# A two-layer attention and gMLP kernel: helper transfers dealt over more steps, and seven stores moved from SP to POOL

## The chip, the cores and the metric

The kernel runs on one core of one Trainium2 chip. The core has five engines with queues of their own: TensorE (PE, matrix products; PEld is its loading of weights), VectorE (DVE), ScalarE (ACT), GpSimd (POOL) and SyncE (SP, which here only issues transfers). Transfers between DRAM and on-chip memory run on 16 DMA engines; an engine's queue issues them in its own order. POOL issues transfers too, among them those that add into what lies at the destination.

The metric is the device time of one execution in microseconds (us), as the median of several runs.

## The reference

Input is x, 2048 tokens by 512. Each of two layers, with the same weights, does a linear attention and a gated MLP whose gate mixes the tokens:

```python
x = x + A(layernorm(x))     # twice: A, B, A, B
x = x + B(layernorm(x))

def B(x):                                   # D = 512, Fh = 896, S = 2048
    z = gelu(x @ w_in)                      # [S, 2*Fh]
    z1, z2 = z[:, :Fh], layernorm(z[:, Fh:])
    g = w_sp @ z2 + b_sp[:, None]           # w_sp is [S, S]
    return (z1 * g) @ w_out
```

A projects to q, k and v in 32 heads of 16, applies `phi(t) = t+1 if t>0 else exp(t)`, sums k with v over all tokens, multiplies with q, divides by the normaliser and projects with wo. The change touches the mixing product `w_sp @ z2`, the storing of z1 and the transfers around them.

## The kernel before, in words

**Arithmetic.** Every fp32 product is made of three matmuls on a high part and a low part (L163 to L165 and L1484 to L1486: high by high, high by low, low by high). The high part is a rounded copy (type fp32r), the low part is what is left. For a piece of w_sp the copy is made on ACT (L1316) and the subtraction on DVE (L1317).

**Stages.** Each layer runs: layernorm, keys, values and their sums; a transition; a pass over the tokens that ends in x @ w_in and the gelu; then the mixing product with the gates, and the output product with w_out. The pages of z1 = gelu(x @ w_in1), 7 for each of four chunks of 512 tokens, are stored to DRAM (L991) and loaded again when the gates need them.

**The mixing product** is written in seven half-size products in place of eight: P2, P1, P6, P7, P4, P5, P3, in this order, 8 steps each. A step multiplies with one piece of w_sp of 512 KB, or with a sum of pieces. Some of these products are divided once more by the same scheme: P4 in layer one, P2 and P4 in layer two. A divided product has 14 steps of 12 matmuls: seven inner products 1, 5, 6, 2, 7, 3, 4 in two halves each (steps 0 and 1 are inner product 1, steps 2 and 3 inner product 5, and so on).

**What each step does.** `run` (L1786 and after) goes through the steps g. In step g:
- `fetch(g + 4)` issues the load of a piece on SP. A plain piece comes from w_sp itself (L1296, `qd<-in_wsp_dram`), an inner product's sum from the DRAM tiles hP (L1296, `qd<-hP`), an outer sum from the tiles s (L1301, `qd<-s`).
- `sp(g + 2)` splits the piece of step g + 2 (L1316 on ACT, L1317 on DVE). ACT's instruction is kept as `mark`.
- `mm(g)` issues the matmuls.
- one gate, where one is due, is issued (`tick`), a copy or an add of the list PARTS (`halve`), and, at the ends of products, the sums are taken out of PSUM by DVE (`evac`, `evac_div`).

A tile of a piece (raw) and its two parts (high and low together) come out of six slots, `qd`. A slot is free when the last reader is done: DVE's subtraction for the raw piece, the matmuls for the parts. So SP's next load often waits for a subtraction of DVE.

**Copies and adds for the sums.** hP holds the sums of pieces that the divided products need: for P4 and for P2, inner products 1, 3, 2 and 4 in two halves q. `halve(n)` does part n of 32, in layer one only: parts 0 to 7 are the copies for P4 (products 1, 3, 2, 4, two halves each), 8 to 15 the adds for P4 in the same order, 16 to 23 the copies for P2, and 24 to 31 its adds. A copy is a transfer of 512 KB from DRAM to DRAM, issued by SP (L1217). An add is an adding transfer of 512 KB, issued by POOL (L1221) behind `mark`. The adds for products 2 and 4 read hP of products 1 and 2. `PARTS` says at which step of which product each part is issued. The sums of P4 are used in the same layer, in its own P4; those of P2 and P4 are used again in layer two.

**The start of the mixing product in layer two.** The x @ w_in products of the last chunk (n = 3) run on into `run`: `while p2.f()` issues them, seven of them, each with its gelu into a page out of the pool `pg` (L988) and its store by SP (L991). After the fourth, `sp(1)` and `fetch(3)` are called. `loadb` loads four pages of b_sp (L1515) at step 0 of the mixing product in layer two, and at step 3 in layer one. The four slots `bg` serve as the sums gb[0] to gb[3], one for each chunk; in P2 the first sum written into gb[3] is that of inner product 5, behind step 3.

**The output stage** (`out7`) has eight rounds j. In each PE multiplies with parts of w_out, ACT and DVE take out the results, and `ofinish` adds pages of them into x by POOL's adding transfers (L1704). In layer one, `join_a` and `join_b` start layer two's loads and layernorm meanwhile (L133 loads its weights and x).

Of the kernel before, what the change touches and what calls it, by code (L numbers as in the profile page):

```python
# [15 lines left out]
P = 128  # L16
# [4 lines left out]
NCHK = S // 512  # L21
NF = FH // P
# [40 lines left out]
EXTRA = (2, 3, 4, 5, 16, 17)  # L63
WSTORE = 9
FS = {6: 1, 12: 1, 17: 1}
PARTS = {("P1", k): k - 2 for k in range(2, 8)} | {("P6", k): 6 + k for k in range(8)}
PARTS |= {("P7", 0): 14, ("P7", 1): 15} | {("P4", 2 * k): 16 + k for k in range(7)}
PARTS |= {("P4", 13): 23} | {("P5", k): 24 + k for k in range(8)}


class Sheets:
# [18 lines left out]
def mixer_kernel(ctx: ExitStack, tc: tile.TileContext, x_in, wqkv, wo_d, win1_d, win2_d, wsp_d, bsp_d, wout_d,  # L90
                 ident_d, mask_d, out_d):
    nc = tc.nc
# [7 lines left out]
    pages = Slots(main, "pg", 22)  # L100
    quads = Slots(main, "qd", 6)
    bigs = Slots(main, "bg", 4)
# [5 lines left out]
    def ztag(i, shape, kind, dtype=F32):  # L108
        t = main.tile(shape, dtype, tag=f"z{i}", bufs=1, name=f"z{i}_{kind}")
        ztile[i] = t  # L110
        return t
# [17 lines left out]
    z1s = {}  # L129
# [37 lines left out]
    class Weight:  # L167


        def __init__(self, slots, shape, pieces, turned=False):  # L170
            self.slots, self.shape, self.pieces, self.turned = slots, shape, pieces, turned
            self.h = self.l = None
            self.raw = deque()
            self.n_load = self.n_split = 0
# [147 lines left out]
    class ZHome:  # L322
# [3 lines left out]

        def get(self, shape, dtype=F32):
            return ztag(self.i, shape, "y" if dtype == F32 else "q", dtype)

        def put(self, t):  # L330
            pass
# [361 lines left out]
    class P2:  # L693
# [288 lines left out]
        def fout(self):  # L982
            if self.fdone is None:
                return
            b, n, f, home = self.fdone
            self.fdone = None
            t = home.get(PAGE)
            nc.scalar.activation(t, b, AF.Gelu_apprx_tanh)  # L988
            banks.put(b)
            z1s[self.L, n, f] = dram.tile(PAGE, F32, name=f"z1_{self.L}_{n}_{f}")  # L990
            nc.sync.dma_start(z1s[self.L, n, f], t)  # L991
            home.put(t)

        def run(self, sums):
# [260 lines left out]
    class P4:  # L1255
# [471 lines left out]
        def out7(self, nxt):  # L1727

            V = nc.vector
            lo, hi = slice(0, 256), slice(256, 512)  # L1730
            last = HT - 1
            u, y, z = self.begun
            for j in range(HT):
                if j == last - 1 and nxt is None:
                    self.loadx(NT - 2)
                    self.loadx(NT - 1)
                d, s = banks.get(PAGE), pages.get(PAGE)
                c = s[:, lo]
                more = j < last
                if more:  # L1740
                    self.opart(j + 1)
                    self.ohigh(0, 1, 2)
                    self.olow(0, 1, 2)
                    if j:
                        self.omul(z, 2, u[:, lo], False, True)
                    self.omul(z, 5, u[:, hi], False, True)
                    if j == 0:
                        self.omul(z, 2, u[:, lo], False, True)
                    nc.scalar.activation(c, u[:, hi], AF.Copy)
                    self.osum(1, 3)  # L1750
                else:
                    self.omul(z, 2, u[:, lo], False, True)
                if nxt is not None:
                    self.join_a(j, nxt)
                self.omul(z, 6, y[:, lo], False, False)
                nc.scalar.activation(d[:, lo], y[:, lo], AF.Copy)
                if more:
                    up, yp, zp = self.pair(j + 1)
                else:
                    self.omul(z, 5, u[:, hi], False, True)  # L1760
                    nc.scalar.activation(c, u[:, hi], AF.Copy)
                V.tensor_add(y[:, lo], y[:, lo], c)
                if more:
                    self.osum(2, 4)
                    self.ohigh(3)
                self.omul(z, 7, d[:, lo], False, False)
                V.tensor_add(d[:, hi], d[:, lo], c)
                pages.put(s)
                if more:
                    self.olow(3)  # L1770
                if j == 0:
                    self.evac("P3", (1,))
                for _ in range((0, 2, 1, 1, 2)[j] if j < 5 else 0):
                    self.tick()
                if nxt is not None:
                    self.join_b(j, nxt)
                self.omul(z, 3, y[:, lo], False, True)
                if more or nxt is not None:
                    self.omul(z, 4, d[:, lo], False, True)
                    self.ofree(z)  # L1780
                self.olone(j, 0, u[:, lo], lo)
                self.olone(j, 0, y[:, lo], hi)
                self.olone(j, 1, d)
                if more or nxt is not None:
                    self.ofinish(2 * j, (u[:, lo], lo), (y[:, lo], hi))
                    self.ofinish(2 * j + 1, (d, slice(0, 512)))  # L1786
                    banks.put(u, y, d)
                    pages.put(self.ones.pop(j))
                    if j % 2 == 0 and more:
                        bigs.put(self.gb[j // 2])  # L1790
                if more:
                    u, y, z = up, yp, zp
            if nxt is not None:
                return
            self.omul(z, 4, d[:, lo], False, True)
            self.olast(NT - 2, u[:, lo], lo)
            self.olast(NT - 2, y[:, lo], hi)
            self.olast(NT - 1, d[:, hi], hi)
            self.olast(NT - 1, d[:, lo], lo)
# [8 lines left out]
        def run(self, nxt):  # L1808
            p2 = self.p2
            self.fetch(2)  # L1810
            self.sp(0)
            self.zmade = 0
            if self.div:
                self.zahead(1)
            early = nxt is None
            n = 0
            while p2.f():
                self.zahead(min(self.zmade, 3))
                n += 1
                if early and n == 4:  # L1820
                    self.sp(1)
                    self.fetch(3)
            self.zahead(3)
            if p2.win1 is not None:
                p2.win1.free()
            if not early:
                self.sp(1)
                self.fetch(3)
            self.gb = [bigs.get([P, NF, 512]) for _ in range(NCHK)]
            n = len(self.steps)  # L1830
            for g in range(n):
                p, k = self.steps[g]
                self.fetch(g + 4)
                evac_first = (p == "P6" or p == "P1" and nxt is not None) and k == HT - 1
                div_first = p in self.div and k == 13 and p == "P4"
                if not evac_first and not div_first:
                    self.sp(g + 2)
                    self.zahead(g + 4 if p in ("P2", "P1") else g + 4)
                self.mm(g)
                if evac_first:  # L1840
                    if p == "P1":
                        self.ask(3)
                    self.evac(p)
                    self.sp(g + 2)
                self.sums.tick()
                if nxt is not None:
                    self.sums.halve(PARTS.get((p, k), -1), self.mark)
                if g == (0 if early else 3):
                    self.loadb()
                if p in self.div:  # L1850
                    if k % 2 == 1:
                        self.evac_div(p, self.SEVEN[k // 2])
                    if div_first:
                        self.sp(g + 2)
                    if k == 13 and p == "P4":
                        self.gq.extend((n, f) for n in range(2) for f in range(3))
                    continue
                if p == "P1" and k == 6:
                    self.ask(3)
                self.tick()  # L1860
                if p == "P3":
                    if k == FIRST:
                        self.first()
                self.wseven(p, k)
                if p == "P7" and k == HT - 1 and self.div:
                    self.sp(g + 3)
                if k == HT - 1 and not evac_first:
                    self.evac(p, (0,) if p == "P3" else (0, 1))
            pages.put(*self.bs)
            self.out7(nxt)  # L1870
# [34 lines left out]
    for L in range(2):  # L1905
        p1.run(sums)
        p2 = P2(p1)
# [5 lines left out]
        nxt = P1(1) if L == 0 else None  # L1913
# [33 lines left out]
```

## Time and profile before

| what | us |
|---|---|
| median of 3 runs | 1366.25 |
| lowest and highest run | 1366.12, 1369.26 |
| profiled execution, device time | 1368.58 |
| its span, first to last instruction | 1366.7 |
| busy PE, PEld | 1356.0, 1153.0 |
| busy DVE, ACT, POOL | 982.1, 695.6, 424.6 |

The profile is of one execution. In its rows a line such as L1317 is a line of the kernel before, `out<-in` names tiles, and `x7` counts instructions. A row of the timeline gives the start and the duration in us; brackets give the idle time just before and what ended it. PE is one after the other in matmuls whose stated durations overlap, so the distance between their starts tells its pace. A row of a wait gives total, times and longest. A DMA row gives the times from issue to landing.

### The profile page before, as it was taken

What the parts mean: (1) busy time and instruction counts of PE and PEld (TensorE: products, weight loads), DVE (VectorE), ACT (ScalarE), POOL (GpSimd) and SP (SyncE); (2) the same over time, 40 slices, a digit from 0 to 9 for tenths busy, and PEclk for the clock granted to TensorE, in tenths of its full rate; (3) what the DMA queues carried; (4) which work ended last, traced back from release to release, by engine and by line L of the source; (5) the groups of instructions that cost most, each with busy time, mean ns of one, the idle gap of its engine ahead of it and who ended that gap; (6) DMA issues with size and microseconds to landing.
All of it is one profiled execution on the core that took longest, in us unless ns stands there. A gap on an engine that the chain in (4) does not pass through costs nothing.

```text
span 1366.7 us, 18857 instructions
## 1 busy us (share of the span) xinstructions
PE 1356.0 (99%) x6602; PEld 1153.0 (84%) x6602; DVE 982.1 (72%) x1550; ACT 695.6 (51%) x1152; POOL 424.6 (31%) x573
## 2 busy tenths in 40 slices
PE   9999999999999999999999999999999999999998
PEld 7888888888888787889988888888887888888898
DVE  6665867762474688898866777777537768888985
ACT  5764534434322355354676655556676333644454
POOL 3753355444350400301322333545330022011021
PEclk9999999999999999999999999999999999999999
DMA  5872257877996968973664423678767445464444
GB/s 181 271 243 95 89 186 261 284 263 242 313 317 222 275 188 273 262 237 68 143 159 131 122 87 99 205 246 260 227 196 230 149 162 163 143 193 154 147 75 65
DMA packets 155022, 260.63 MB, mean 191 GB/s; under 512 B 13104, under 2 KB 52272, under 8 KB 154672
## 3 DMA queue, kind: packets, MB, share of 16 engines
q1 hardware_dynamic: 140240, 228.50, 50.6%
q0 software_dynamic: 14688, 30.94, 11.4%
q8 instruction: 51, 0.84, 0.2%
q14 instruction: 43, 0.35, 0.1%
HBM read 187.83 MB, written 88.34 MB: 202 GB/s over the span
## 4 chain that ended last, share of the span: by engine, by line
PE 75%; DVE 4%; DMA 3%; ACT 2%; issue 1%; POOL 0%; DVEq 0%; SPq 0%; ACTq 0%; POOLq 0%
PE bank L1484 11%; PE bank L1485 11%; PE bank L1486 11%; PE bank L165 9%; PE bank L163 9%; PE bank L164 9%; PE bank L1682 3%; PE bank L1683 3%; PE bank L1684 3%; PE bank L849 1%; PE bank L848 1%; PE bank L847 1%; DVE qd L1317 1%; DMA qd<-hP 1%; DMA pg<-z 1%
## 5 line engine op out<-in xcount | busy, mean ns | idle before, releaser
L1484 PE MATMUL bank<-qd,pg 128*128 128x512 f32 x776 | 302.4, 390 | 2.2 <-ACT pg L1354 1.8
L1485 PE MATMUL bank<-qd,pg 128*128 128x512 f32 x776 | 302.2, 389 | 1.4 <-DVE qd L1317 1.4
L1486 PE MATMUL bank<-qd,pg 128*128 128x512 f32 x776 | 302.1, 389 | 0.0
L1317 DVE TENSOR_TENSOR qd<-qd,qd 128x1024 fp32r<-128x1024 f32 x130 | 164.4, 1265 | 122.4 <-ACT qd L1316 122.4
L1316 ACT ACTIVATE qd<-qd 128x1024 fp32r<-128x1024 f32 x130 | 137.3, 1056 | 186.7 <-PE bank L1486 119.7
L165 PE MATMUL bank<-qd,pg 128*128 128x512 f32 x496 | 193.5, 390 | 0.3 <-DVE pg L152 0.3
L1484 PEld LDWEIGHTS bank<-qd,pg 128*128 128x128 f32 x776 | 145.6, 188 | 34.1 <-ACT pg L1354 2.6
L1485 PEld LDWEIGHTS bank<-qd,pg 128*128 128x128 f32 x776 | 145.7, 188 | 32.1 <-DVE qd L1317 2.1
L1486 PEld LDWEIGHTS bank<-qd,pg 128*128 128x128 f32 x776 | 145.7, 188 | 31.0 <-DVE pg L1356 0.7
L163 PE MATMUL bank<-qd,pg 128*128 128x512 f32 x356 | 138.8, 390 | 0.0
L164 PE MATMUL bank<-qd,pg 128*128 128x512 f32 x356 | 138.7, 390 | 0.0
L1525 POOL TENSOR_TENSOR bg<-bg,pg 128x512 f32<-128x512 f32 x28 | 51.4, 1837 | 246.5 <-ACT qd L1316 203.7
L165 PEld LDWEIGHTS bank<-qd,pg 128*128 128x128 f32 x496 | 93.1, 188 | 20.6 <-DVE pg L152 1.2
L298 POOL TENSOR_SCALAR rs<-mv 128x1 f32<-128x1 f32 x80 | 24.4, 304 | 214.8 <-DVE mv L296 213.3
L307 ACT ACTIVATE pg<-pg,nb,rs 128x512 f32<-128x512 f32 x52 | 42.1, 810 | 88.0 <-POOL nb L301 87.4
L1684 PE MATMUL bank<-wo,qd 128*128 128x256 f32 x288 | 81.4, 283 | 0.0
L1231 POOL TENSOR_TENSOR pg<-pg,pg 128x512 f32<-128x512 f32 x48 | 68.6, 1428 | 36.4 <-DMA pg<-in_wsp_dram 19.6
L164 PEld LDWEIGHTS bank<-qd,pg 128*128 128x128 f32 x356 | 66.8, 188 | 14.0 <-DVE qd L152 0.3
L163 PEld LDWEIGHTS bank<-qd,pg 128*128 128x128 f32 x356 | 66.8, 188 | 13.8 <-ACT pg L149 0.2
L1682 PE MATMUL bank<-wo,qd 128*128 128x256 f32 x276 | 78.1, 283 | 0.0
L1683 PE MATMUL bank<-wo,qd 128*128 128x256 f32 x276 | 78.0, 283 | 0.0
L1354 ACT ACTIVATE pg<-pg 128x384 fp32r<-128x384 f32 (+1 forms) x32 | 18.5, 579 | 84.6 <-DVE pg L1352 47.6
(224 smaller groups left out, 3071.8 us busy)
## 6 DMA issues: line engine op xcount, KB each, us to landing
qd<-s SPq DMA_DIRECT2D x64, 512.0 KB, 3.7
qd<-in_wsp_dram SPq DMA_DIRECT2D x42, 512.0 KB, 4.3
pg<-z SPq DMA_DIRECT2D x56, 256.0 KB, 4.0
pg<-w POOLq DMA_DIRECT2D x56, 256.0 KB, 4.9
pg<-in_wsp_dram SPq DMA_DIRECT2D x48, 256.0 KB, 5.0
z<-pg SPq DMA_DIRECT2D x48, 256.0 KB, 3.3
s<-pg SPq DMA_DIRECT2D x48, 256.0 KB, 4.4
qd<-hP SPq DMA_DIRECT2D x24, 512.0 KB, 3.8
```

Source lines behind the costliest of these rows:

```text
L163: nc.tensor.matmul(out, ah, bh, start=start, stop=False)
L164: nc.tensor.matmul(out, ah, bl, start=False, stop=False)
L165: nc.tensor.matmul(out, al, bh, start=False, stop=stop)
L1231: nc.gpsimd.tensor_tensor(t, a, b, op=OP.add)
L1316: self.mark = nc.scalar.activation(w[:, 0], r, AF.Copy)
L1317: nc.vector.tensor_sub(w[:, 1], r, w[:, 0].bitcast(F32))
L1484: m(out, h[:, o], w[:, 0, j, :], start=start, stop=False, skip_group_check=True)
L1485: m(out, h[:, o], w[:, 1, j, :], start=False, stop=False, skip_group_check=True)
L1486: m(out, l[:, o], w[:, 0, j, :], start=False, stop=stop, skip_group_check=True)
L1682: m(out, A, x, start=start and f == 0, stop=False, skip_group_check=True)
L1683: m(out, A, y, start=False, stop=False, skip_group_check=True)
L1684: m(out, B, x, start=False, stop=stop and f == 2, skip_group_check=True)
```

## The change

Three things change, and no transfer, matmul or other operation is added or taken away.

- `PARTS`: the 32 parts of copies and adds are dealt out anew. Parts 0 to 5 stay at P1's steps 2 to 7. Before, P6 had one part at each of its 8 steps, P7 one at steps 0 and 1, P4 one at steps 0, 2, 4, 6, 8, 10, 12 and 13, P5 one at each of its 8 steps. After, P6, P7 and P5 have one at steps 0, 2, 4 and 6, P4 one at the same steps as before, and the output stage one in each of the rounds 1 to 6. So the copies of P4's product 4 stand at P6's steps 0 and 2; the adds of product 1 at P6's 4 and 6, of product 3 at P7's 0 and 2, of product 2 at P7's 4 and 6, of product 4 at P4's 0 and 2; the copies for P2 at P4's 4, 6, 8, 10, 12, 13 and P5's 0 and 2; the adds for P2's product 1 at P5's 4 and 6, and the other six in the output stage.
- In layer two the last seven gelus write seven sheets of one `bg` slot (class `Spare`) in place of pages out of `pg`, and their stores are issued by POOL. The slot goes back before the four sums take their slots, and becomes gb[3].
- In layer two `loadb` moves from step 0 of the mixing product to the place behind the fourth of the last gelus, right after `fetch(3)`.

```diff
-PARTS = {("P1", k): k - 2 for k in range(2, 8)} | {("P6", k): 6 + k for k in range(8)}
-PARTS |= {("P7", 0): 14, ("P7", 1): 15} | {("P4", 2 * k): 16 + k for k in range(7)}
-PARTS |= {("P4", 13): 23} | {("P5", k): 24 + k for k in range(8)}
+PARTS = {}
+for p, ks in (("P1", range(2, 8)), ("P6", (0, 2, 4, 6)), ("P7", (0, 2, 4, 6)), ("P4", (0, 2, 4, 6, 8, 10, 12, 13)),
+              ("P5", (0, 2, 4, 6)), ("out", range(1, 7))):
+    for k in ks:
+        PARTS[p, k] = len(PARTS)
...
+    class Spare:
+
+        def __init__(self, t):
+            self.t, self.n = t, 0
+
+        def get(self, shape):
+            self.n += 1
+            return self.t[:, self.n - 1]
 
         def put(self, t):
             pass
...
             z1s[self.L, n, f] = dram.tile(PAGE, F32, name=f"z1_{self.L}_{n}_{f}")
-            nc.sync.dma_start(z1s[self.L, n, f], t)
+            (nc.gpsimd if self.L and n == NCHK - 1 else nc.sync).dma_start(z1s[self.L, n, f], t)
             home.put(t)
...
                 if nxt is not None:
                     self.join_b(j, nxt)
+                if nxt is not None:
+                    self.sums.halve(PARTS.get(("out", j), -1), self.mark)
                 self.omul(z, 3, y[:, lo], False, True)
...
             early = nxt is None
             n = 0
-            while p2.f():
+            spare = Spare(bigs.get([P, NF, 512])) if early else pages
+            while p2.f(home=spare):
                 self.zahead(min(self.zmade, 3))
                 n += 1
                 if early and n == 4:
                     self.sp(1)
                     self.fetch(3)
+                if early and n == 4:
+                    self.loadb()
...
+            if early:
+                bigs.put(spare.t)
             self.gb = [bigs.get([P, NF, 512]) for _ in range(NCHK)]
...
-                if g == (0 if early else 3):
+                if g == 3 and not early:
                     self.loadb()
```

More of the change, by code (lines that the diff above doesn't have):

```diff
@@ L328, in get, with put @@
             return ztag(self.i, shape, "y" if dtype == F32 else "q", dtype)
+        def put(self, t):
+            pass
+    class Spare:
[4 more added lines that the diff above has]
+            return self.t[:, self.n - 1]
         def put(self, t):
```

## The prediction

> **What bounds the kernel now.** I read the page first: its busy shares, the DMA slices and the groups. Then I asked for the waits of TensorE (PE), because they say what could be gained at all.
>
> ```profile
> span 1366.7 us, 18857 instructions
> PE 1356.0 (99%) x6602; PEld 1153.0 (84%) x6602; DVE 982.1 (72%) x1550; ACT 695.6 (51%) x1152; POOL 424.6 (31%) x573
> PE bank L542 <- DVE pg L537: 2.3, 1, 2.3
> PE bank L1484 <- ACT pg L1354: 1.8, 2, 1.1
> PE bank L1485 <- DVE qd L1317: 1.4, 2, 0.8
> ```
>
> PE is busy 99% of the span, so any change to transfers gains only from the few moments when PE waits. The columns of the waits are total, times and longest. L542 belongs to the start, which the diff doesn't touch. The rest are the spatial steps: layer one's (L1354) and layer two's (L1317, DVE's split of a w_sp piece). The two waits on L1317 lie in layer two's P2, at its steps 5 and 6. The timeline of PE shows them:
>
> ```profile
> 1040.48 0.39 PE L1484 MATMUL bank<-qd,pg 128*128 128x512 f32 x1
> 1040.71 0.39 PE L1485 MATMUL bank<-qd,pg 128*128 128x512 f32 x1
> ...
> 1041.23 0.49 PE L1484 MATMUL bank<-qd,pg 128*128 128x512 f32 x1
> 1042.49 0.50 PE L1485 MATMUL bank<-qd,pg 128*128 128x512 f32 x1 [0.77 <-DVE qd L1317]
> ...
> 1046.16 0.50 PE L1485 MATMUL bank<-qd,pg 128*128 128x512 f32 x1 [0.65 <-DVE qd L1317]
> ...
> 1048.81 0.39 PE L1484 MATMUL bank<-qd,pg 128*128 128x512 f32 x1
> ```
>
> The stated duration of one matmul (0.39) overlaps the next, so the pitch of the starts counts: 0.227 us (1040.48, 1040.71). A step of a divided product has 12 matmuls, 2.72 us. From 1041.23 to 1048.81 run two steps, 24 matmuls: 7.58 us for 24 x 0.227 = 5.44, so **2.14 us are lost** there. The marked idle (1.4) understates it, since the matmuls around a wait are late too.
>
> Why is the split late? The chain that ended last, in order of time, goes back through two loads to a gelu:
>
> ```profile
> 1021.52 2.01 DMA z<-pg
> ...
> 1025.70 1.24 DVE qd L1317
> 1026.95 4.13 DMA qd<-hP
> ...
> 1033.29 6.72 DMA qd<-hP
> 1040.11 1.07 ACT qd L1316
> ```
>
> A z1 page is stored (z<-pg), the next gelu waits for the page to come free, ACT's copy of step 1's piece stands behind that gelu, DVE's subtract behind the copy, and the freed slot is what the load of step 3 takes at 1026.95. Step 5's load starts at 1033.29 and takes 6.72 us. These are the rows that show how late each link is:
>
> ```profile
> 1023.63 1.09 ACT L988 ACTIVATE pg<-bank 128x512 f32<-128x512 f32 x2 [1.29 <-DMA z<-pg]
> 1027.42 1.42 SPq L991 DMA_DIRECT2D z<-pg  x3
> 1029.81 3.44 SPq L1515 DMA_DIRECT2D pg<-in_bsp_dram  x4
> 1029.34 1.23 DVE L1317 TENSOR_TENSOR qd<-qd,qd 128x1024 fp32r<-128x1024 f32 x1 [2.41 <-ACT qd L1316]
> 1041.21 1.23 DVE L1317 TENSOR_TENSOR qd<-qd,qd 128x1024 fp32r<-128x1024 f32 x1 [3.13 <-ACT qd L1316]
> 1055.71 1.22 DVE L1317 TENSOR_TENSOR qd<-qd,qd 128x1024 fp32r<-128x1024 f32 x1
> 1026.95:1040.01 13.06, 13.06 (x59) 10.82 (x58) 6.22 (x9) 6.42 (x11) 0.00 (x0) 1.00 0.90 296
> ```
>
> **Part B, layer two's last seven z1 pages.** Seven gelus write sheets of one spare slot, POOL issues the seven stores, and the four loads of b_sp pages go ahead of step 4's fetch. It adds and removes no byte.
>
> First link: the gelu's 1.29 us of waiting goes, since no sheet is used twice. ACT's copy of step 1 then starts some 1.3 us earlier and step 3's fetch at about 1026.95 - 1.3 = 1025.6. Second link: three stores (1.42 us of issue) and the four b_sp loads (3.44) leave SP's queue between that and step 5's fetch. The slot this fetch takes is free at 1029.34 + 1.23 = 1030.57, so it may go 1033.29 - 1030.57 = 2.7 us earlier.
>
> How soon does it land? The last row above, a window, gives, in order, the stretch, its length, busy time of the five engines, clock, DMA share 0.90 and 296 GB/s: from 1026.95 to 1040.01 the transfer engines are nearly full. Two readings bound it.
> - If an earlier issue is worth its full 2.7 us, the piece lands near 1037.3, ACT adds 1.1 (1040.11 to 1041.21), and the split starts near 1038.4.
> - If the bytes bind, the same bytes start 1.3 us earlier and end 1.3 earlier: 1038.7, and the split starts near 1039.8.
>
> When must it start? Without a stall step 5 begins at 1041.2 and its second matmul 0.23 later, so its own split may end at 1041.4 and start at 1040.2. But DVE then works without a pause: step 10's split ends at 1055.71 + 1.22 = 1056.93, 15.7 us after 1041.21, while PE's five steps take 13.6. So the stream has to start by 1041.16 + 13.6 - 15.7 = 1039.05. By the first reading all 2.14 us come back, by the second it starts 0.75 too late and 2.14 - 0.75 = 1.4 come back. I take the middle, **-1.8 us**. The bounds are 0 (next rival) and -2.2.
>
> On POOL the seven issues stand behind its last work of that phase and in front of nothing until the gates, so their price falls on no other instruction. POOL's issues in this trace, and the stores' own landing while SP issues them:
>
> ```profile
> L991 SPq DMA_DIRECT2D z<-pg x7: 320/332/438, 1019.5 to 1028.4; - x7
> DMA to landing us min/median/max: 2.0/2.2/4.6
> L1221 POOL DMA_DIRECT2D hP<-in_wsp_dram x8: 809/834/1077, 449.0 to 565.0; - x8
> ```
>
> (ns, least, median, most.) Issue on POOL is dearer, 0.8 against 0.33 us, but the sheets aren't written again until the spare slot takes the fourth group of sums, behind P2's step 3, that is at 1041.16 - 2.72 = 1038.4. The last store, issued near 1028.4 as now, would have to take 10 us to be late.
>
> Here a rule of the Trainium skill speaks against the change: page "SBUF — State Buffer", section "SBUF: two separate sides", says that a transfer issued from GpSimd has its descriptors written by GpSimd itself, and that this is locked out while VectorE runs certain two-port operations. The trace shows POOL's adding transfers issued in 809 to 1077 ns in stages where DVE is busy throughout, which is no sign of such a lock. By the rule the stores would drift into step 5's load, and the sum for this part would be near 0.
>
> **Part A, layer one's copies and adds.** 32 parts before and after: 16 copies by SP, 16 adding transfers by POOL. The copies and adds for P4 spread from P6 and two steps of P7 over P6, P7 and P4's first steps. Six adds for layer two's P2 leave P5 for the output stage. Again nothing is added. How full the transfer engines are in each stage (P6, P7, P4, output):
>
> ```profile
> 439.00:472.40 33.40, 33.03 (x146) 27.03 (x145) 20.92 (x25) 11.27 (x15) 14.80 (x13) 1.00 0.91 267
> 472.40:506.30 33.90, 33.15 (x144) 26.98 (x145) 29.89 (x55) 14.95 (x22) 2.39 (x3) 1.00 0.68 196
> 506.30:544.40 38.10, 38.10 (x169) 31.34 (x167) 34.30 (x54) 22.93 (x34) 0.00 (x0) 1.00 0.80 273
> 622.50:694.40 71.90, 71.90 (x573) 70.54 (x573) 59.36 (x100) 44.30 (x82) 18.79 (x23) 1.00 0.61 122
> ```
>
> P6, where the first adds crowd, has a DMA share of 0.91, and the change moves transfers to stages at 0.68, 0.80 and 0.61. But the crowding costs PE nothing now. L1354's 1.8 us are one wait of 0.7 in P7, behind P6's sums, which the order of the program sets, and one of 1.1 at P5's first step. Behind that one the chain has this load:
>
> ```profile
> 535.38 6.48 DMA qd<-s
> ```
>
> It runs beside copies that SP issues at P4's steps 8, 10 and 12; before and after, a copy stands at each of these. So I count **0** there, bound -1.1, the wait itself.
>
> The other side is P4's own loads. The first row below is the time from issue to landing (least, median, most) of P6's loads of w_sp pieces, with adds beside them, the second that of P4's loads, without. Then come ACT's copies of P4's steps 4 and 7, DVE's split of step 7 and the first matmul of step 7.
>
> ```profile
> DMA to landing us min/median/max: 3.3/9.0/12.4
> DMA to landing us min/median/max: 3.5/3.8/5.6
> 514.33 1.05 ACT L1316 ACTIVATE qd<-qd 128x1024 fp32r<-128x1024 f32 x1
> 520.54 1.06 ACT L1316 ACTIVATE qd<-qd 128x1024 fp32r<-128x1024 f32 x1 [0.76 <-DMA qd<-in_wsp_dram]
> 523.31 1.22 DVE L1317 TENSOR_TENSOR qd<-qd,qd 128x1024 fp32r<-128x1024 f32 x1
> 525.35 0.39 PE L1484 MATMUL bank<-qd,pg 128*128 128x512 f32 x1
> ```
>
> The last m4 add, dealt to P4's step 2, is held behind ACT's copy of step 4, so it issues near 514.33 + 1.05 = 515.4, beside the loads of steps 6 to 8. Step 7's copy ends at 521.60, DVE takes it 1.7 us later and ends at 524.53, PE needs it at 525.35: the cover is 1.7 + 0.8 = 2.5 us. At P6's least there is no loss; at its median 9.0 - 3.8 - 2.5 = +2.7 us; at its most +6.1. I take the value of P4 itself, 0, since one add is in flight there, and a copy that ran beside the same loads goes.
>
> In the output stage an add per step stands beside the loads of layer two's weights. SP's row of their issues, their landing times and ACT's first use:
>
> ```profile
> 667.79 5.22 SPq L133 DMA_DIRECT2D pg<-in_wqkv_dram  x8
> DMA to landing us min/median/max: 5.3/8.2/8.9
> 675.45 0.62 ACT L149 ACTIVATE qd<-pg 128x512 fp32r<-128x512 f32 x1
> ```
>
> The first lands at 667.79 + 5.3 = 673.1 and is used 2.35 us later. Stretched to P6's median it would be 9.0 - 5.3 - 2.35 = +1.3 late; these loads already take up to 8.9, so I take 0. For its issues POOL has 71.90 - 18.79 us idle.
>
> **Sum.** The profiled execution took 1368.58 us (span 1366.7 and 1.9 around it): 1368.58 - 1.8 + 0 = 1366.8. It lies 2.3 above the median of the runs, 1366.25, so there: 1366.25 - 1.8 = **1364.4 us**, 0.13% less. About 0.3% (4.1 us: 1362.15 and 1370.35) is what can be told from no change.
>
> **Rivals.**
> - *Part B gives nothing*: the stores only change queue, step 5's load shares full engines with the same bytes and still lands at 1040, or POOL's stores land later and beside it. For it: DMA share 0.90 in that window. Against it: the load that heads the queue there starts 1.3 us earlier, and nothing is added. 1366.2 us.
> - *The P5 load is freed too*, because fewer transfers are outstanding on the way to it: -1.1 more, 1363.3. Against: the same three copies stand beside it.
> - *Slower*: the m4 add stretches P4's loads, where DVE has no idle time to catch up. It decides as soon as a load there takes more than 3.8 + 2.5 + 1.8 = 8.1 us, which P6's median exceeds. Price +2.7 to +6.1, middle 4.4: 1366.25 + 4.4 - 1.8 = 1368.9. Against: one add at a time, and P4's DMA share of 0.80 leaves room.
> - *The change doesn't do what it says*, that is, the gelus find another wait (the spare slot taken late): the same 1366.2 as the first rival, counted with it.
>
> **How the numbers follow.** Forecast 0.52 (own range 1363.6 to 1365.6), part B nothing 0.17, P5 freed 0.12, slower 0.19. The range goes from 1362.0 (both gains in full, 1366.25 - 2.2 - 1.1 = 1362.95, and 0.95 more, since runs scatter: from 0.13 below the median to 3.0 above) to 1369.2, past the slower rival's middle. Faster by over 0.3%: a tenth of the forecast and three quarters of the P5 case, if its load frees more behind it, 0.14. Slower by over 0.3%: the upper half of the slower rival and a little scatter, 0.12. Within: 0.74.
>
> **What would show it.** Right: no wait of PE for DVE's split in layer two's P2, the gelus there wait for PE alone, step 3's load issued near 1025.6, step 5's landing by 1038.7. Wrong: a wait of PE in layer one's P4 or in the output stage (slower rival), a P5 first load under 5 us (second), or step 5's load landing at 1040 (first).

## The result, and the profile after

The changed kernel is **slower by 0.2%**: 1368.86 us, median of 22 runs (1367.36 to 1372.89), against 1366.01 us (22 runs, 1364.13 to 1369.26) for the kernel before. The ratio is 1.0020, interval 1.0013 to 1.0026. The forecast was 1364.4 us, so the time moved the other way.

In the changed kernel line numbers are 2 higher up to the helpers (L163 is L165) and 14 higher behind `Spare` (L1317 is L1331; in experiments with the old `PARTS` it is L1329). The largest waits of PE over the whole run, total, times and longest:

```profile
PE bank L556 <- DVE pg L551: 2.3, 1, 2.3
PE bank L1696 <- ACT bg L151: 1.9, 1, 1.9
PE bank L1498 <- ACT pg L1368: 0.8, 1, 0.8
```

The waits for DVE's split in layer two are gone, and the 1.8 us for ACT's copy (L1354 before) are down to 0.8. A new wait of 1.9 us has come: L1696 is a matmul of the output stage, and L151 is ACT's copy of an operand.

A wait alone doesn't tell what it costs. For the table below, the distance from each matmul's start to the next is taken, less the usual distance for its shape, and added up by stretch. It is the time that PE lost, in us. The usual distance is a low one, so a stretch of 30 us without any wait still shows about 0.1, and the whole run some 5. "B alone" and the like are experiments told below.

| stretch of the span | before | changed | B alone | P4's adds in P6 and P7 only |
|---|---|---|---|---|
| 471 to 505, P7 | 1.89 | 0.10 | 1.66 | 0.10 |
| 505 to 541, P4 | 0.11 | 0.80 | 0.11 | 0.47 |
| 541 to 590, P5 | 1.94 | 1.71 | 0.32 | 0.37 |
| 620 to 692, output stage | 0.25 | 4.41 | 0.26 | 0.26 |
| 1000 to 1055, layer two's P2 | 2.39 | 0.40 | 0.54 | 0.62 |
| whole run | 20.71 | 20.95 | 15.68 | 15.01 |

P7 and layer two's P2 gained 3.8 us, the output stage lost 4.2, P4 0.7. The totals of before and changed come out near each other, while the medians differ by 2.85 us. For 1.55 us of this the reason is plain: the profiled execution of before took 1368.58 us, 2.57 above its median of 22 runs, that of the changed kernel 1369.88, 1.02 above. Another 0.7 lies outside the span of the instructions (1.88 us before, 2.58 changed), and no run here shows why. Some of the stalls in the first column aren't there in every execution: "B alone" runs the same layer one and lost 0.32 us in P5, not 1.94.

**The output stage.** The first two rows are windows of 14 us over the same matmuls, of the kernel before and of the changed one, which is 2.0 us ahead here (length, busy time of PE, PEld, DVE, ACT and POOL, clock, DMA share, GB/s). The others are of the changed kernel: POOL's adds, SP's loads of layer two's weights, the time of these loads from issue to landing, and what ACT and PE waited for.

```profile
663.00:677.00 14.00, 14.00 (x114) 13.82 (x113) 11.27 (x19) 9.27 (x17) 3.78 (x5) 1.00 0.89 188
661.00:675.00 14.00, 14.00 (x114) 13.82 (x113) 11.27 (x19) 8.15 (x14) 5.61 (x7) 1.00 0.97 183
```

```profile
661.23 0.95 POOL L1235 DMA_DIRECT2D hP<-hP  x1
662.97 1.91 POOL L1235 DMA_DIRECT2D hP<-hP  x1
...
665.79 12.44 SPq L135 DMA_DIRECT2D pg<-in_wqkv_dram  x8
DMA to landing us min/median/max: 7.6/12.3/12.6
678.44 0.63 ACT L151 ACTIVATE qd<-pg 128x512 fp32r<-128x512 f32 x1 [4.89 <-DMA pg<-in_wqkv_dram]
680.56 0.39 PE L1696 MATMUL bank<-wo,bg 128*128 128x256 f32 x1 [1.91 <-ACT bg L151]
```

The eight loads took 5.3 to 8.9 us before and take 7.6 to 12.6 now. The transfer engines were nearly full here before the change too, at a share of 0.89: the 0.61 that the prediction went by is the mean of the whole stage. ACT's queue has its copy of the first weight piece in front of the copy that PE's next matmul needs (L151, `bg`). So ACT stands 4.89 us for a load whose data nobody needs yet, and PE stands 1.91 us behind it. The Trainium skill, page "DMA: Bandwidth & Descriptors", section "Issuing engines are not separate DMA queues", says that transfers run on the same 16 engines and interleave whichever engine issued them; the later landing, at a share of 0.97 in place of 0.89, agrees.

Then something comes on top that the prediction didn't have. The windows of the changed kernel behind the wait:

```profile
678.00:682.00 4.00, 2.00 (x15) 1.60 (x13) 1.98 (x3) 3.56 (x9) 2.71 (x4) 1.00 1.08 358
682.00:684.00 2.00, 2.00 (x12) 1.65 (x10) 1.97 (x6) 0.46 (x2) 0.57 (x1) 0.66 1.04 243
684.00:686.00 2.00, 2.00 (x10) 1.97 (x10) 1.33 (x3) 0.94 (x1) 0.00 (x0) 0.50 1.13 216
686.00:688.00 2.00, 2.00 (x18) 2.00 (x18) 1.43 (x1) 2.00 (x4) 0.00 (x0) 0.99 1.12 218
```

The granted clock (third number from the end) falls to 0.50 some 2 us after the wait, for about 3.4 us. In 684 to 686 PE does 10 matmuls, in 686 to 688 18. Of the 4.41 us, the wait makes 2.06 and the stretch at 0.50 about 1.7. It isn't in every execution: the mean clock of the whole run is 0.998 in 9 of the 22 runs, this one among them, and 1.000 in 9 others. The medians of these two groups are 1368.9 and 1368.6 us, so the slower clock is not what makes the change slow.

**Layer two's P2.** Where the links of the prediction's chain stand now. Of before: the first matmul of step 0 and DVE's split for step 4. Of the changed kernel: two gelus, step 3's load, the first matmul of step 0, the loads of steps 4 and 5, and the splits for steps 4 and 5.

```profile
1027.56 0.39 PE L1484 MATMUL bank<-qd,pg 128*128 128x512 f32 x1
1036.18 1.23 DVE L1317 TENSOR_TENSOR qd<-qd,qd 128x1024 fp32r<-128x1024 f32 x1 [2.10 <-ACT qd L1316]
```

```profile
1024.51 1.07 ACT L1002 ACTIVATE bg<-bank 128x512 f32<-128x512 f32 x2
1027.81 0.36 SPq L1310 DMA_DIRECT2D qd<-hP  x1
1029.80 0.39 PE L1498 MATMUL bank<-qd,pg 128*128 128x512 f32 x1
1030.58 2.63 SPq L1310 DMA_DIRECT2D qd<-hP  x2
1039.41 1.23 DVE L1331 TENSOR_TENSOR qd<-qd,qd 128x1024 fp32r<-128x1024 f32 x1 [3.60 <-ACT qd L1330]
1041.48 1.23 DVE L1331 TENSOR_TENSOR qd<-qd,qd 128x1024 fp32r<-128x1024 f32 x1 [0.17 <-ACT qd L1330]
```

The two executions are best compared by the time from step 0's first matmul. The gelu row carries no wait for a store any more. Step 3's load went 0.61 us ahead of that matmul (1026.95 against 1027.56) and now goes 1.99 ahead: 1.38 earlier. The split of step 5 started 13.65 us behind it (1041.21) and now starts 11.68 behind (1041.48): 1.97 earlier. The split of step 4, whose load now stands behind those of b_sp, starts 0.99 later (8.62 and 9.61 behind).

### The profile page after: what moved, and what is told of

Its sections match the earlier page's. It is cut to its first block, busy times and chain, and to the rows that moved or that the text cites. A ratio compares the mean times of both kernels' runs of the same rounds, so it can differ in the third digit from the quotient of the medians.

```text
span 1367.3 us, 18852 instructions
## 1 busy us (share of the span) xinstructions
PE 1357.1 (99%) x6602; PEld 1153.8 (84%) x6602; DVE 981.7 (72%) x1550; ACT 695.3 (51%) x1152; POOL 432.4 (32%) x580
## 3 DMA queue, kind: packets, MB, share of 16 engines
q0 software_dynamic: 15248, 32.77, 11.9%
## 4 chain that ended last, share of the span: by engine, by line
PE 90%; DVE 3%; DMA 2%; ACT 2%; issue 1%; POOL 1%; SPq 0%; DVEq 0%; ACTq 0%; POOLq 0%
PE bank L167 13%; PE bank L165 13%; PE bank L166 13%; PE bank L1498 12%; PE bank L1500 12%; PE bank L1499 12%; PE bank L1696 3%; PE bank L1698 3%; PE bank L1697 3%; PE bank L863 1%; PE bank L861 1%; PE bank L862 1%; DMA qd<-in_wsp_dram 1%; DMA pg<-in_wqkv_dram 1%; PE bank L680 1%
## 5 line engine op out<-in xcount | busy, mean ns | idle before, releaser
L1331 DVE TENSOR_TENSOR qd<-qd,qd 128x1024 fp32r<-128x1024 f32 x130 | 162.8, 1253 | 117.2 <-ACT qd L1330 117.1
L1539 POOL TENSOR_TENSOR bg<-bg,pg 128x512 f32<-128x512 f32 x28 | 55.6, 1986 | 277.0 <-ACT qd L1330 200.6
L165 PE MATMUL bank<-qd,pg 128*128 128x512 f32 x356 | 139.1, 391 | 0.5 <-DVE pg L154 0.3
L165 PEld LDWEIGHTS bank<-qd,pg 128*128 128x128 f32 x356 | 66.8, 188 | 14.9 <-DVE pg L154 0.9
L1696 PE MATMUL bank<-wo,qd 128*128 128x256 f32 x276 | 78.1, 283 | 0.0
```

The lines of the kernel that those rows point to most:

```text
L165: nc.tensor.matmul(out, ah, bh, start=start, stop=False)
L1331: nc.vector.tensor_sub(w[:, 1], r, w[:, 0].bitcast(F32))
L1696: m(out, A, x, start=start and f == 0, stop=False, skip_group_check=True)
```

## The experiments

Theory 1: the six adds in the output stage make the change slow, through the weight loads and ACT's queue; everything else gains. Rivals: P4's adds (theory 2, the slower rival of the prediction), or part B (theory 3). Each kernel was timed beside the kernel before on the same chip; ratios are to that one, intervals in brackets. Layer one's PARTS are given as in the diff above.

**Part B alone** (the changed kernel with the old `PARTS` and without `halve` in `out7`).

> Part B alone (spare sheets, POOL's stores, b_sp loads earlier), layer one's copies and adds as before. Theory 1 (the output stage's adds make the loss, all else gains): PE's starts at layer two's P2 lose 0.4 us instead of 2.4, as in the changed kernel, so 1366.0 - 2.0 = 1364.0 us. Theory 2 (the loss is in layer one's P4, where the last adds meet the loads): the same 1364.0. Theory 3 (part B itself costs outside the profile): 1366 or more.

1364.37 us, ratio 0.9991 (0.9982 to 1.0000). Part B gains about 1.2 us; theory 3 falls.

**Part A alone** (the kernel before with the new `PARTS` and `halve` in `out7`).

> Part A alone (copies and adds dealt over every other step and the output stage), layer two as before. Theory 1: the changed kernel without part B's gain, 1368.9 + 2.0 = 1370.9 us, with a wait of PE of about 2 us in the output stage and a granted clock below 1 right after it. Theory 2: about 1370.9 too, but with the lost time in P4. Theory 3: at most 1367.

1369.18 us, ratio 1.0025 (1.0014 to 1.0036). PE waited 1.5 us for L151 in the output stage, and the clock fell to 0.50 behind it. Theory 1 had 1370.9, so the size was overstated; the place was right.

**No adds in the output stage:**

```diff
-              ("P5", (0, 2, 4, 6)), ("out", range(1, 7))):
+              ("P5", range(8)), ("P3", (0, 2))):
```

> The changed kernel with the six adds of the output stage back in P5 (its odd steps) and P3 (steps 0 and 2). Theory 1: the output stage loses nothing, P7's gain of 1.8 us and part B's of 2.0 stay, P4 costs about 0.6: 1366.0 - 1.8 - 2.0 + 0.6 = 1362.8 us. Theory 2: no better than the changed kernel, 1368 to 1369. Theory 3: 1365 or more.

1365.49 us, ratio 1.0000 (0.9991 to 1.0009). The output stage lost 0.26 us, like before: the change's loss is gone. But the 3 us of gain that theory 1 summed up aren't there; it had taken them from the profile of before, which was 2.57 us above its median. As built, this kernel has P5's two copies at steps 0 and 1 and adds at 2 to 7.

**P4's adds over P6 and P7 alone:**

```diff
-("P7", (0, 2, 4, 6)), ("P4", (0, 2, 4, 6, 8, 10, 12, 13)), ("P5", (0, 2, 4, 6)), ("out", range(1, 7))
+("P7", range(6)), ("P4", (0, 2, 4, 6, 8, 10, 12, 13)), ("P5", range(8))
```

> Part B, and of part A only the adds for P4 dealt over P6's steps 4 and 6 and P7's steps 0 to 5; copies for P2 in P4 and adds for P2 in P5 as before, none in P4 or the output stage. Theory 1: 1366.0 - 1.8 - 2.0 = 1362.2 us, 0.6 better than with adds in P4. Theory 2: 1362.2 as well, and then several us better than the kernel with adds in P4 and none in the output stage.

1363.59 us, ratio 0.9987 (0.9979 to 0.9996): faster than both kernels, though 1.4 us above the forecast sum, whose gains came from the same profile. Between 440 and 760 us PE has no marked wait at all.

**Rounds 3 and 4 kept free** (`("out", (0, 1, 2, 5, 6, 7))`).

> The changed kernel with its six output-stage adds in rounds 0, 1, 2, 5, 6, 7 in place of 1 to 6, so that none is issued in rounds 3 and 4, just ahead of layer two's first weight loads. Theory 1 (two adds beside these loads make the first one 12.6 us instead of 5.3, and ACT's copy of it holds up what PE needs): the wait of 1.9 us and the clock below 1 behind it go, the first weight load lands within 9 us, and the time is that of the kernel without output-stage adds, 1365.4 us. Rival (any add in this stage costs, through POOL's queue and the adding stores of x): still 1368 to 1369.

1371.25 us, ratio 1.0039 (1.0025 to 1.0053): worse than the changed kernel, and neither of the two values that were forecast. The mechanism still shows. The weight loads are early again, and the adds of rounds 5 to 7 now lie beside the loads of layer two's first transposed x (L135, `xt`). The rows are the weight loads' times to landing, that of one such load of x, issued at 684, PE's wait at layer two's first matmuls, and a window at the lower clock:

```profile
DMA to landing us min/median/max: 4.0/7.6/9.2
...
DMA to landing us min/median/max: 13.4/13.4/13.4
...
698.96 0.80 PE L165 MATMUL bank<-qd,pg 128*128 128x512 f32 x1 [3.43 <-ACT pg L151]
698.00:704.00 6.00, 5.04 (x12) 3.94 (x13) 3.37 (x7) 5.43 (x10) 2.85 (x5) 0.50 0.44 56
```

PE lost 0.25 us in the output stage and 6.46 at the start of layer two. So here an add costs where a load with a short lead is beside it, be it one of weights or of x. The clock was at 0.50 for 6.8 us, from 1.4 us before this wait ended. Behind another wait, of 1.61 us at P5's first step (543.96), it stayed at 1.00.

**ACT's first weight copy a round later:**

```diff
-                for _ in range(j - 4):
+                for _ in range(0 if j == 5 else 3):
                     nxt.wk.piece()
```

> The changed kernel, all adds in their places; only ACT's copy of the first weight piece moves from round 5 to round 6, with the two that stand there. Theory 1: the weight load still takes 12 us, but ACT no longer waits for it in front of PE's operands: no wait of PE, clock 1, 1365.4 us. Rival (the crowded engines themselves slow the stage): the wait shows up elsewhere in the stage and the time stays at 1368 to 1369.

1366.25 us, ratio 1.0011 (1.0001 to 1.0020). The adds are where the change puts them and the weight loads still take up to 11.9 us, yet about half of the loss is gone by the medians (the intervals overlap), and PE lost 1.55 us in the output stage in place of 4.41: the order on ACT carried a large part. Not all: the next chain is a result page whose adding store is late, in front of another operand:

```profile
686.91 0.60 ACT L1717 ACTIVATE pg<-bank 128x512 f32<-128x512 f32 x1 [2.09 <-DMA x<-pg]
688.36 0.39 PE L1696 MATMUL bank<-wo,bg 128*128 128x256 f32 x1 [1.23 <-ACT bank L1770]
```

So the rival has a part in it: crowded transfers hold up two waiters here, the weight's copy and the result page.

**Part B taken apart**, on part B alone. First with the stores issued by SP (`nc.sync.dma_start(z1s...)` again):

> Part B alone, but with the seven stores issued by SP as before (spare sheets and the earlier b_sp loads stay). If the gelus' wait for their pages was what was late, most of part B's gain stays: 1364.4 to 1365 us and no gelu waits for a store. If SP's queue was, the load of P2's step 5 is issued as late as before and the time is that of before, 1365.4 or more.

1364.6 us, ratio 0.9996 (0.9988 to 1.0005); PE waited 0.6 us in P2. Some of the gain may go, too little to measure. Then with POOL's stores but recycled pages (`spare = pages`):

> Part B alone, but with the gelus writing recycled pages as before (POOL's stores and the earlier b_sp loads stay). If the gelus' wait for their pages was what was late, nothing is gained: step 3's load goes as late as before, 1365.4 us or more. If SP's queue was, the gain stays: 1364.4 us.

1367.29 us, ratio 1.0012 (1.0003 to 1.0021): worse than before. The gelus wait again, and step 3's load goes at the start of step 0's first matmul, no longer ahead of it. PE loses 4.71 us in P2, and the chain behind its wait goes to DVE, which needs a page whose store, issued at 1026.50, took 6.68 us to land. ACT's and DVE's rows, PE's wait and a window behind it:

```profile
1021.45 1.09 ACT L1000 ACTIVATE pg<-bank 128x512 f32<-128x512 f32 x2 [1.89 <-DMA z<-pg]
...
1025.61 1.58 ACT L1000 ACTIVATE pg<-bank 128x512 f32<-128x512 f32 x3 [2.13 <-DMA z<-pg]
...
1033.38 0.76 DVE L1393 TENSOR_TENSOR pg<-z_z,pg 128x256 f32<-128x256 f32 x2 [3.99 <-DMA z<-pg]
...
PE bank L1497 <- DVE qd L1329: 2.6, 1, 2.6
1038.00:1040.00 2.00, 2.00 (x6) 1.61 (x5) 2.00 (x4) 1.60 (x4) 0.00 (x0) 0.50 0.58 169
```

And without the move of `loadb` (back at step 0):

> Part B alone without the move of the b_sp loads (they stand behind step 4's fetch again, at step 0). If they were part of what made step 5's load late, about half of part B's gain goes: PE loses 1 to 1.5 us in layer two's P2 in place of 0.5 and 2.4, 1364.8 us. If the gelus' wait was all of it, 1364.2 as with all of part B.

1364.3 us, ratio 0.9986 (0.9977 to 0.9995). As good as all of part B; PE lost 0.94 us in P2. By the profiles the move takes 0.4 us off step 5's split and puts 2.7 on step 4's. The spare slot is what counts.

**P4's last two adds at its steps 1 and 3** (as P4's adds over P6 and P7 alone, with `("P7", (0, 2, 4, 6)), ("P4", (1, 3))` for parts 10 to 15; the copies stay at 0, 2, 4, ...).

> The kernel with P4's adds dealt over P6 and P7 alone, but its last two adds (product 4) at P4's steps 1 and 3. Theory 1: adds beside P4's loads cost 0.4 to 1.9 us: 1364.0 to 1365.5. Rival (the kernel without output-stage adds was no faster than before for its adds in P5 and P3): as without them, 1363.6.

1367.99 us, ratio 1.0015 (1.0006 to 1.0024), more than either theory had. Here copy and add lie beside the same three loads (steps 6 to 8). Their times to landing and PE's two waits:

```profile
DMA to landing us min/median/max: 6.2/8.1/8.6
...
525.28 0.51 PE L1498 MATMUL bank<-qd,pg 128*128 128x512 f32 x1 [0.84 <-ACT qd L1330]
526.54 0.50 PE L1499 MATMUL bank<-qd,pg 128*128 128x512 f32 x1 [0.76 <-DVE qd L1331]
...
528.00:530.00 2.00, 2.00 (x6) 1.58 (x5) 2.00 (x4) 1.64 (x3) 0.00 (x0) 0.50 1.27 500
```

This is the prediction's slower rival, built as a kernel: PE lost 4.08 us in P4. In the changed kernel, where the add takes the place of a copy, it was 0.80.

**Output-stage adds without P4's** (P4's adds over P6 and P7 alone, `("P5", (4, 6)), ("out", range(1, 7))`), **and the changed kernel beside it:**

> The kernel with P4's adds dealt over P6 and P7 alone, and of the adds for P2 the last six in rounds 1 to 6 of the output stage. Theory 1: the output stage alone makes the changed kernel slow: a wait of PE of 1.5 to 2 us, a clock near 0.5 for 3 us behind it, 1363.6 + 4 = 1367.6 us. Rival (the loss needs P4's adds too): at most 1365.

> The changed kernel once more, beside these on one chip. By its earlier runs 1.002 of the kernel before: 1368 us. Theory 1: 0.5 to 2 us above the kernel that has the output-stage adds without P4's.

1368.77 us, ratio 1.0023 (1.0013 to 1.0033), and 1368.76 us, ratio 1.0021 (1.0012 to 1.0029). The output stage alone makes the whole loss. P4's adds, forecast at 0.5 to 2 us more, cost nothing that shows. PE lost 3.13 and 3.21 us in the output stage, and this time the clock, forecast near 0.5, stayed at 1.00 in both: the weight load's copy on ACT waited 4.0 us and more, PE 1.0 and 1.3, and another 0.5 and 0.6 a little later.

**Two questions left, on one chip:** the kernel without output-stage adds again, with its two P4 adds moved to P7 (`("P7", range(6)), ("P4", (4, 6, 8, 10, 12, 13)), ("P5", range(8)), ("P3", (0, 2))`); adds in rounds 0 to 2 alone (`("P5", (1, 3, 5, 7)), ("P3", (4,)), ("out", (0, 1, 2))`); and the best kernel so far once more.

> The kernel without output-stage adds, with its two adds in P4 moved to P7 (steps 4 and 5); copies for P2 at P4's steps 4 to 13 and P5's 0 and 2, adds for P2 in P5 and P3 as there. If the adds in P4 cost the 1.8 us: 1363.6. If the adds in P5 and P3 do: 1365.4.

> P4's adds over P6 and P7, and of the adds for P2 four in P5 (odd steps), one in P3 (step 4), three in rounds 0, 1 and 2 of the output stage. If only adds beside layer two's weight and input loads cost (rounds 3 to 7): 1363.6, and no wait of PE in that stage. If any add there costs: 1366 or more.

> The kernel with P4's adds dealt over P6 and P7 alone and part B, once more, beside the two others: 0.9987 of before, 1363.6 us.

0.9995 (0.9986 to 1.0004), 0.9990 (0.9981 to 0.9998) and 0.9989 (0.9981 to 0.9998). Adds in the first three rounds cost nothing that shows: PE lost 0.25 us in the output stage. The kernel with P4's adds over P6 and P7 and with part B is about 0.1% faster than before again. The first of the three (its P5 is that of the kernel without output-stage adds) lies between the values that would have decided. So whether the two P4 adds or the adds in P5 and P3 cost that kernel its gain stays open; that P4's adds cost nothing beside those of the output stage speaks against them.

## Why the prediction was wrong

- **Part B, -1.8 us: right in mechanism, its size within what can be told.** Step 3's load went 1.38 us earlier (forecast 1.3), step 5's split 1.97 us earlier, between the two readings of 2.7 and 1.3. The medians give -1.2 (interval 0 to -2.5) with part B alone and -1.9 without the `loadb` move. The moved `loadb`, which the prediction counted in the second link, showed no gain of its own, and SP's queue at most a small one. In three later profiles with all of part B PE still lost 1.3, 1.6 and 1.7 us in P2, so the gain isn't whole in every execution.
- **POOL's stores: right.** They were issued in 0.54 us each. The first row is their landing in the changed kernel, the second that of the same stores out of the spare slot when SP issues them (part B taken apart):

```profile
DMA to landing us min/median/max: 2.3/2.5/6.7
...
DMA to landing us min/median/max: 2.0/2.2/7.0
```

  So the slowest is no later from POOL than from SP; out of recycled pages before, it took 4.6.

  The rule of the Trainium skill on descriptors written by GpSimd (page "SBUF — State Buffer", section "SBUF: two separate sides") would have had them late. This trace shows no sign of it. It tests the rule little, though: while they were issued DVE ran nothing but TENSOR_TENSOR, and it was busy 8.43 of the 14 us from 1019 to 1033. Beside POOL's adds, where the prediction has DVE busy throughout, it was busy 20.92 of P6's 33.40 us.
- **"The crowding costs PE nothing now": wrong, by 1.8 us in the profile.** I put the waits in P7 down to the program's order. The trace of before shows ACT's copy waiting for a load; DVE's split stands behind the copy and P6's sums (L1542) behind the split. The third row has the same sums in the changed kernel, 3.27 us earlier, 0.65 of which is its lead at this place:

```profile
466.55 1.06 ACT L1316 ACTIVATE qd<-qd 128x1024 fp32r<-128x1024 f32 x1 [5.25 <-DMA qd<-s]
471.60 3.67 DVE L1542 TENSOR_TENSOR bg<-bank,pg 128x512 f32<-128x512 f32 x6
...
468.33 3.78 DVE L1556 TENSOR_TENSOR bg<-bank,pg 128x512 f32<-128x512 f32 x6
```

  With fewer adds in P6 its loads (`qd<-s`, P7's first among them) land in 3.2, 5.1 and 6.5 us (least, median, most), not 3.3, 9.0 and 12.4, and P7's stall of 1.89 us is 0.10, that is none, in all twelve profiles that deal the adds out. It isn't in every execution of the old `PARTS` either: in the five profiles with them the slowest of these loads took 12.4, 12.2, 10.4, 10.0 and 8.0 us, and PE lost 1.89, 1.66, 1.37, 1.02 and 0.10 us in P7. By the medians the gain is smaller: -0.6 us between part B alone and P4's adds over P6 and P7 (intervals overlap).
- **P5's first load, 0: right in price, but not in mechanism.** The load was freed, 4.9 us in place of 6.5, which the prediction had named as the sign of its second rival. PE still waited 0.8 us in place of 1.1, since ACT now stood for the load ahead of it, a piece of P4's last steps:

```profile
537.65 1.06 ACT L1330 ACTIVATE qd<-qd 128x1024 fp32r<-128x1024 f32 x1 [3.01 <-DMA qd<-in_wsp_dram]
538.91 1.06 ACT L1330 ACTIVATE qd<-qd 128x1024 fp32r<-128x1024 f32 x1 [0.20 <-DMA qd<-s]
```

  So the 0 came true by luck. What PE loses in P5 runs from 0.1 to 2.5 us over all the profiles, and from 0.3 to 2.0 over those with the old `PARTS`.
- **P4's loads, 0 with +2.7 to +6.1 as the bound: near.** They landed in

```profile
DMA to landing us min/median/max: 3.5/5.2/7.4
```

  and PE lost 0.7 us more there, which the medians don't show. The rival's price is real where an add comes on top of a copy (+4.0 us of lost starts), but it didn't decide here.
- **The output stage, 0: this step failed.** The text had the right loads, the lead of 2.35 us and a bound of +1.3, and set it aside with "these loads already take up to 8.9, so I take 0". The first load took 12.6 us. The bound itself was too low, since it took P6's median; P6's most, 12.4, would have given 12.4 - 5.3 - 2.35 = +4.75, near the 4.89 that ACT then waited. And the price was counted for the load's own use, while what stands behind it on ACT's queue is an operand of PE. By the medians the six adds cost 4.6 us (from 0.9989 to 1.0023 of before).
- **The slower clock behind a wait** was no term at all. It makes about 1.7 of the 4.41 us in the first profile of the changed kernel, and nothing in the second, which lost 3.21.
- **The sum** took its gain in full from one execution that was 2.57 us above the median of 22 runs.

With the failed step at its measured size, and part B's and P7's gains by the medians, the sum is 1366.0 - 1.2 - 0.6 + 4.6 = 1368.8, against 1368.86. Its terms come from the experiments, so it shows that the account closes and is no test of it.

## What to carry to other kernels

A transfer that is moved to a stage with idle engines is paid by the loads there with the shortest lead, so look up every load in the new stage, its lead, and what stands behind its first user on that user's queue: a copy that waits early for data needed late blocks what is needed now. When a bound comes from a crowded stage, take its longest load as well as its median, and read how full the transfer engines are over the stretch in which the loads run (0.89 here), not over the stage (0.61). And weigh a stall found in one profiled execution by how that execution stands to the median: some of it may be chance.

## What the runs showed of the hardware

PE's granted clock fell to 0.50 for 3.4 us behind waits of 1.46 us (part A alone), 1.91 (changed), 2.61 (part B with recycled pages) and behind two waits of 0.84 and 0.76 close together (P4's adds at steps 1 and 3), and for 6.8 us around one of 3.43 (rounds 3 and 4 free). It stayed at 1.00 behind waits of 1.0, 1.2 and 1.3 us, behind 0.77 and 0.65 in the kernel before, and behind the 1.61 at P5's first step with rounds 3 and 4 free. So the length of a wait alone doesn't decide it here. The Trainium skill, page "TensorE: Matmul & The Clock Gate", section "What's actually happening", puts the return to half rate at an idle window of about 3.4 us; here idle times well under that were enough in four profiles. With the clock's part, PE lost 4.4, 4.7 and 6.5 us in the stretches around the waits of 1.91, 2.61 and 3.43, about twice the wait.
